# Two corners of causal attention, one product for two heads instead of one for each

## The chip, the cores and the metric

The kernel runs on one core of one Trainium2 chip. The metric is the device time of one execution in microseconds (us); lower is better. Before the change it is 387.51 us, the median of 3 runs (386.67 to 387.80).

The core's engines each work through their own queue in order: TensorE (PE: matrix products, with its weight loads as PEld), VectorE (DVE), ScalarE (ACT), GpSimd (POOL) and SyncE (SP), which issues the DMAs here.

## The reference

Per batch and head (8 x 8 heads, 576 positions, head size 64) causal attention with a decay, then a soft mixture of experts over all 4608 tokens:

```
scores = scale * q @ k^T
cum    = cumsum(log(clip(f, 1e-4, 1)))
scores = where(causal, -1e9, scores + cum_i - cum_j)
attn   = exp(scores - rowmax);  attn /= attn.sum + 1e-9
x      = (attn @ v), heads side by side         # 4608 x 512
logits = x @ phi;  dispatch = softmax over tokens;  combine = softmax over slots
out    = combine @ experts(dispatch^T @ x)      # two layers with relu
```

## The kernel before

**Tiling.** The 64 heads are worked as 32 pairs `g`, 4 pairs to a batch. For a pair, `YA` holds the rounded queries of both heads with extra rows below them (constants, and one row of row maxima), and `WA` the rounded keys with rows of the decay's sums; `YB` and `WB` hold copies and rounding remainders. All in float32r.

**Three stages per head.**

- `s1` and `tops` find each query's largest score. `s1` (L225) puts queries on partitions, blocks of 128 that are shifted by 64: block 0 is 64 blank lanes and the first 64 queries, blocks 1 to 4 are whole. Causality bounds the keys of a block: 64, 192, 320, 448 and 576 (as 2 x 288), six products in four fills of PSUM banks `s` (there are three such banks). `tops` (L238, DVE) adds a mask and reduces each product to a column of `MT`. `mturn` (L248) transposes a pair's ten columns, `mrows` copies them on ACT and sends them by DMA as the row of maxima into `YA`.
- `s2` and `expo` make the weights, with keys on partitions. `SEGS` lists six segments of a head: key blocks 0, 1, 2 with 320, 448, 320 queries, block 0 again with 256, block 3 with 192, and block 4 with 64 keys and 64 queries. Each is two products (L275 with `WA`/`YA`, L276 with the remainders). Four of the segments open a bank of `ring` (three banks); the last three share one. `expo` (L282, ACT) writes the exponentials of a bank to `PT`, and `causal` (L290, L293, POOL) clears the triangles.
- `s3` (L308) multiplies the weights with V, 50 products per pair, each seen twice in the trace; `norm` divides.

**Order.** It is written out by hand: the code's order is each engine's order. Iteration `g` of the main loop (g = 1 to 31) does `s2` for heads h0 = 2g and h1 = 2g+1, between them `s1` and `tops` for u0 = 2g+3 (second head of pair g+1) and u1 = 2g+4 (first head of pair g+2), the transposes of pair g-1, and at its end `s3` of pair g. So a row maximum is made a pair ahead of its use. POOL makes remainders (`low_q`, `low_k`) and the triangles. Every fourth iteration adds the batch's logits (L380), every fourth the dispatch (L461). Weights of the experts are loaded behind it; the tail after the loop computes the experts and stores the output.

**Before the loop** pair 0 and the first half block work of pairs 1 and 2 run with waits between engines, among them `both` (that is `s2` and `expo` of one bank) and `first` (`s1` and `tops`).

Of the kernel before, what the change touches and what calls it, by code (L numbers as in the profile page):

```python
# [41 lines left out]
SEGS = (  # L42
    (0, 1, 128, 448),
    (1, 0, 0, 320),
    (2, 2, 256, 320),
    (3, 0, 320, 256), (3, 3, 384, 192), (3, 4, 512, 64),
)
SEG_O = (640, 0, 320, 1088)


def pt_col(c, i):
    at = {}
    for bank, cc, i0, w in SEGS:
        o = at.get(bank, 0)
        at[bank] = o + w
        if cc == c and i0 <= i < i0 + w:
            return SEG_O[bank] + o + i - i0
    raise ValueError


def queries(t, u):
# [4 lines left out]
HALF = [  # L66
    [(h, t, u, c) for h in range(2) for t in ((4, 3, 2, 1, 0), (0, 1, 2, 3, 4))[h] if t < 4 or u == h for c in range(queries(t, u) // 2 + 1)]
    for u in range(2)
]
VALUES = [x for n in range(25) for h in HALF for x in h[n : n + 1]]  # L70

@with_exitstack
def attn_softmoe(ctx: ExitStack, tc: tile.TileContext, qk, v, f, phi, w1, w2, cst, out):
# [12 lines left out]
    cumd = dram.tile([2, NG, 2, S], F32, name="cumd")  # L86
# [5 lines left out]
    mask = fr[1].tile([P, 448], F32, name="mask")  # L92
    YA, WA, YB, WB = {}, {}, {}, {}
    for n, m in enumerate((1, 0, 2)):
        YA[m] = fr[n].tile([P, 2, 640], F32R, name=f"YA{m}")
        WA[m] = fr[n].tile([P, 2 * S], F32R, name=f"WA{m}")
        if m < 2:
            YB[m] = fr[n].tile([P, 2, S], F32R, name=f"YB{m}")
            WB[m] = fr[n].tile([P, 2 * S], F32R, name=f"WB{m}")
    RAW = [per.tile([P, 2, S], F32, name=f"RAW{i}") for i in range(3)]  # L100
    PTS = per.tile([P, 3200], F32, name="PTS")
    PT = [PTS[:, 1600 * i : 1600 * i + 1600] for i in range(2)]
# [12 lines left out]
    MT = [const.tile([P, 2 * NBLK], F32, name=f"MT{i}") for i in range(3)]  # L115
# [33 lines left out]
    def pair(g):  # L149
        return 0 <= g < NG  # L150
# [29 lines left out]
    def round_q(g, *hs):  # L180
        if pair(g):
            for h in hs or range(2):
                nc.scalar.copy(YA[g % 3][0:64, h, 64:640], RAW[g % 3][0:64, h])  # L183

    def load_cum(g):
        if pair(g):
            r0, r1 = CUM[g % 3]
            dst = WA[g % 3][r0 : r1 + 1 : r1 - r0, 0 : 2 * S].rearrange("c (h s) -> c h s", h=2)
            nc.sync.dma_start(dst.bitcast(F32), cumd[:, g].rearrange("h c s -> c h s"))
# [6 lines left out]
    def dup_q(g, h0=0, h1=2):  # L196
        if pair(g):
            nc.sync.dma_start(YB[g % 2][0:64, h0:h1].bitcast(F32), YA[g % 3][0:64, h0:h1, 64:640].bitcast(F32))
# [7 lines left out]
    def low_q(i):  # L206
        if head(i):
            g, h = divmod(i, 2)
            nc.gpsimd.tensor_tensor(YB[g % 2][64:128, h], RAW[g % 3][0:64, h], YA[g % 3][0:64, h, 64:640].bitcast(F32), op=ALU.subtract)  # L209


    TOPS = ((0, 0, 2, 0, 320), (0, 320, 1, 0, 192), (1, 0, 4, 0, 288), (2, 0, 4, 288, 288), (3, 0, 3, 0, 448), (3, 448, 0, 0, 64))

    def s1(i, *which):
# [4 lines left out]
        ya, wa, m = YA[g % 3], WA[g % 3][:, S * h : S * h + S], TOP[g % 3]  # L219
        for n in which:  # L220
            bank, o, blk, j0, w = TOPS[n]
# [3 lines left out]
            nc.tensor.matmul(  # L225
                t[:, o : o + w], ya[0:m, h, 128 * blk : 128 * blk + 128], wa[0:m, j0 : j0 + w], start=True, stop=True
            )

    def tops(i, *which):
# [3 lines left out]
        for n in which:  # L233
            bank, o, blk, j0, w = TOPS[n]
            t = st["top", i % 2, bank]
            m0 = max(448 - (128 * blk + 64) + j0, 0)
            top = MT[g % 3][:, NBLK * h + blk : NBLK * h + blk + 1] if g else m2[h][:, blk, 1:2]
            nc.vector.tensor_tensor_reduce(  # L238
                out=t[:, o : o + w], in0=t[:, o : o + w], in1=mask[:, m0 : m0 + w], scale=1.0, scalar=top if n == 3 else -3.0e38,
                op0=ALU.add, op1=ALU.max, accum_out=top,  # L240
            )

    def mturn(g, h0=0, h1=2):
# [4 lines left out]
        nc.tensor.transpose(pm[0 : NBLK * (h1 - h0), 0:128], MT[g % 3][:, NBLK * h0 : NBLK * h1], ident)  # L248
        st["pm", g, h0] = pm

    def mrows(g, h0=0, h1=2):
# [3 lines left out]
        n = NBLK * (h1 - h0)  # L255
        mr = small.tile([2 * NBLK, P], F32R, name=f"mr{g}_{h0}", tag="mr", bufs=1)
        nc.scalar.copy(mr[0:n], st["pm", g, h0][0:n, 0:128])  # L257
        m = TOP[g % 3]
        dst = YA[g % 3][m : m + 1, h0:h1].rearrange("c h s -> c (h s)")
        nc.sync.dma_start(dst.bitcast(F32), mr[0:n].bitcast(F32))  # L260

    def s2(i, *which):
# [4 lines left out]
        for n in which:  # L267
            bank, c, i0, w = SEGS[n]
            t, at = (turn(), 0) if n < 4 else st["bank"]

            n = 128 if c < 4 else 64
            o = t[0:n, at : at + w]
            at += w
            j0 = S * h + 128 * c
            nc.tensor.matmul(o, wa[0:m, j0 : j0 + n], ya[0:m, h, 64 + i0 : 64 + i0 + w], start=True, stop=False)  # L275
            nc.tensor.matmul(o, wb[:, j0 : j0 + n], yb[:, h, i0 : i0 + w], start=False, stop=True)  # L276
# [7 lines left out]
    def causal(i):  # L284
# [3 lines left out]
        pt = PT[i % 2]  # L288
        d3 = pt[:, 0:960].rearrange("p (a b) -> p a b", b=320)[:, :, 0:128]
        nc.gpsimd.affine_select(d3, d3, pattern=[[0, 3], [1, 128]], compare_op=ALU.is_ge, fill=0.0, base=0, channel_multiplier=-1)  # L290
        for o, w in ((pt_col(3, 384), 128), (pt_col(4, 512), 64)):
            dd = pt[:, o : o + w]
            nc.gpsimd.affine_select(dd, dd, pattern=[[1, w]], compare_op=ALU.is_ge, fill=0.0, base=0, channel_multiplier=-1)  # L293
# [9 lines left out]
    def s3(g, values):  # L303

        for h, t, u, c in values:
            r = queries(t, u)
            at = pt_col(c, 64 * r)
# [771 lines left out]
```

## Time and profile before

| | |
|---|---|
| median of 3 runs | 387.51 us |
| profiled execution | 386.95 us |
| its span, first to last instruction | 385.2 us |
| PE busy | 94% of the span |
| DVE, ACT, POOL busy | 73%, 69%, 67% |
| mean granted clock | 0.984 |

The profile is of one execution, whose own time is 1.75 us longer than the span. Busy shares are averages over the start (about 27 us), the loop and a tail from about 330 us on, in which the weights stream in at some 400 GB/s. PE's products overlap in a pipeline and their ends are modelled, so the chain of waits, which counts from end to end, says better than a mean duration what one product costs.

### The profile page before, as it was taken

The numbers are of one execution on the slowest core, as the hardware profiler recorded it, in microseconds if no ns is written. First come the engines' busy times: TensorE is split into PE (matmuls) and PEld (weight loads), VectorE is DVE, ScalarE is ACT, GpSimd is POOL, SyncE is SP. The second block draws the span as 40 slices with busy tenths as digits, with TensorE's granted clock in tenths as the row PEclk, the third lists the DMA queues.
The fourth block names the chain that finished last, engine by engine and source line by source line (L and its number), as shares of the span: only waits on it lengthen the run. The fifth ranks groups of instructions, "written<-read, shape, count | busy, mean of one in ns | idle before, by whom it ended". The sixth has DMA issues, their size and how long they took to land.

```text
span 385.2 us, 15103 instructions
## 1 busy us (share of the span) xinstructions
PE 362.4 (94%) x5795; PEld 325.5 (84%) x5795; DVE 281.0 (73%) x1133; ACT 266.2 (69%) x671; POOL 258.7 (67%) x378
## 2 busy tenths in 40 slices
PE   8989999999999999999999999999999998998940
PEld 7879999999999999999999999999999875443620
DVE  7778887889788978888888788878978443412741
ACT  8887787878787878787878778787876553011631
POOL 3887888878878888788878887888788621000000
PEclk9999999999999999999999999999999999999985
DMA  6875667687868777777777777868675799999997
GB/s 207 223 159 156 180 188 208 188 239 223 261 183 254 219 229 213 222 216 215 217 217 216 215 224 212 229 208 236 208 188 154 258 365 378 409 406 403 346 359 300
DMA packets 35144, 93.72 MB, mean 243 GB/s; under 512 B 4234, under 2 KB 10048, under 8 KB 35072
## 3 DMA queue, kind: packets, MB, share of 16 engines
q1 hardware_dynamic: 35072, 92.75, 77.4%
q8 instruction: 46, 0.75, 0.8%
q14 instruction: 26, 0.21, 0.2%
HBM read 63.93 MB, written 9.73 MB: 191 GB/s over the span
## 4 chain that ended last, share of the span: by engine, by line
PE 84%; DMA 9%; DVE 1%; ACT 1%; SPq 1%; issue 1%; DVEq 0%; ACTq 0%
PE pv L308 24%; PE ring L275 15%; PE ring L276 13%; PE s L225 13%; DMA w<-in_w 5%; PE pv L334 4%; PE lg L380 2%; DMA out<-p 2%; PE ds L461 2%; PE ring L498 2%; DMA YA<-mr 2%; PE more L894 1%; PE pv L894 1%; PE pv L498 1%; PE pv L931 1%
## 5 line engine op out<-in xcount | busy, mean ns | idle before, releaser
L282 ACT ACTIVATE PTS<-ring 128x320 f32<-128x320 f32 (+2 forms) x256 | 118.6, 502 | 46.2 <-PE ring L276 39.2
L238 DVE CUSTOM_DVE_ANT_0 s<-s,mask 128x320 f32<-128x320 f32 (+4 forms) x320 | 138.1, 452 | 7.1 <-PE s L225 2.1
L275 PE MATMUL ring<-YA,WA 67*128 67x320 f32 (+9 forms) x384 | 121.7, 329 | 0.5 <-DMA YA<-mr 0.5
L276 PE MATMUL ring<-YB,WB 128*128 128x320 f32 (+4 forms) x384 | 110.5, 296 | 0.0
L308 PE MATMUL pv<-V,PTS 128*64 128x65 f32 x3200 | 101.7, 223 | 0.4 <-ACT mr L257 0.3
L308 PEld LDWEIGHTS pv<-V,PTS 128*64 128x64 f32 x3200 | 96.9, 138 | 3.2 <-issue 0.9
L204 POOL TENSOR_TENSOR WB<-RAW,WB 64x576 fp32r<-64x576 f32 x64 | 90.4, 1414 | 11.8 <-ACT YA L183 5.6
L225 PE MATMUL s<-WA,YA 66*128 66x288 f32 (+9 forms) x384 | 96.3, 306 | 0.5 <-DVE MT L238 0.3
L209 POOL TENSOR_TENSOR YB<-RAW,YA 64x576 fp32r<-64x576 f32 x64 | 89.8, 1421 | 2.5
L275 PEld LDWEIGHTS ring<-YA,WA 67*128 67x128 f32 (+3 forms) x384 | 69.1, 181 | 5.7 <-issue 1.6
L276 PEld LDWEIGHTS ring<-YB,WB 128*128 128x128 f32 (+1 forms) x384 | 69.9, 182 | 0.0
L225 PEld LDWEIGHTS s<-WA,YA 66*128 66x128 f32 (+1 forms) x384 | 64.0, 190 | 3.7 <-DVE MT L238 0.5
L238 DVE DVE_READ_ACCUMULATOR2_ANT MT<- 128x1 f32 x372 | 52.8, 142 | 0.0
L293 POOL TENSOR_SCALAR_AFFINE_SELECT PTS<-PTS 128x128 f32<-128x128 f32 (+1 forms) x128 | 31.5, 268 | 25.8 <-ACT PTS L282 23.0
L178 ACT CAST WA<-RAW 64x576 fp32r<-64x576 f32 x64 | 40.0, 669 | 6.9 <-DMA RAW<-in_qk 6.3
L290 POOL TENSOR_SCALAR_AFFINE_SELECT PTS<-PTS 128x384 f32<-128x384 f32 x64 | 33.4, 522 | 13.8 <-ACT PTS L282 8.7
L183 ACT CAST YA<-RAW 64x576 fp32r<-64x576 f32 x64 | 40.1, 670 | 0.5
L238 DVE CUSTOM_DVE_ANT_0 s<-s,mask,MT 128x288 f32<-128x288 f32 x62 | 32.6, 526 | 9.6 <-PE s L225 0.9
L334 PE MATMUL pv<-cs,X 128*128 128x128 f32 x155 | 37.0, 273 | 0.6 <-DVE X L327 0.6
L327 DVE TENSOR_TENSOR X<-pv,rl 128x320 f32<-128x320 f32 (+1 forms) x65 | 31.6, 487 | 2.4 <-DMA YA<-mr 0.3
L322 DVE TENSOR_SCALAR rl<-pv 128x5 f32<-128x5 f32 x64 | 10.5, 164 | 25.0 <-PE pv L308 24.3
L369 ACT COPY XT<-pv 128x128 f32<-128x128 f32 (+1 forms) x93 | 25.0, 307 | 0.6 <-PE pv L334 0.6
(184 smaller groups left out, 345.7 us busy)
## 6 DMA issues: line engine op xcount, KB each, us to landing
w<-in_w SPq DMA_DIRECT2D x46, 512.0 KB
RAW<-in_qk SPq DMA_DIRECT2D x31, 576.0 KB
V<-in_v SPq DMA_DIRECT2D x32, 325.0 KB
WB<-WA SPq DMA_DIRECT2D x31, 288.0 KB
YB<-YA SPq DMA_DIRECT2D x31, 288.0 KB
p<-in_w SPq DMA_DIRECT2D x7, 512.0 KB
out<-RAW SPq DMA_DIRECT2D x12, 256.0 KB
out<-p SPq DMA_DIRECT2D x5, 512.0 KB
```

Source lines behind the costliest of these rows:

```text
L178: nc.scalar.copy(WA[g % 3][0:64, S * h : S * h + S], RAW[g % 3][64:128, h])
L183: nc.scalar.copy(YA[g % 3][0:64, h, 64:640], RAW[g % 3][0:64, h])
L204: nc.gpsimd.tensor_tensor(t[0:64], RAW[g % 3][64:128, h], t[64:128].bitcast(F32), op=ALU.subtract)
L209: nc.gpsimd.tensor_tensor(YB[g % 2][64:128, h], RAW[g % 3][0:64, h], YA[g % 3][0:64, h, 64:640].bitcast(F32), op=ALU.subtract)
L225: nc.tensor.matmul(t[:, o : o + w], ya[0:m, h, 128 * blk : 128 * blk + 128], wa[0:m, j0 : j0 + w], start=True, stop=True)
L238: nc.vector.tensor_tensor_reduce(out=t[:, o : o + w], in0=t[:, o : o + w], in1=mask[:, m0 : m0 + w], scale=1.0, scalar=top if n == 3 else ...
L275: nc.tensor.matmul(o, wa[0:m, j0 : j0 + n], ya[0:m, h, 64 + i0 : 64 + i0 + w], start=True, stop=False)
L276: nc.tensor.matmul(o, wb[:, j0 : j0 + n], yb[:, h, i0 : i0 + w], start=False, stop=True)
L282: nc.scalar.activation(PT[i % 2][:, SEG_O[bank] : SEG_O[bank] + at], t[:, 0:at], AF.Exp, scale=0.125)
L290: nc.gpsimd.affine_select(d3, d3, pattern=[[0, 3], [1, 128]], compare_op=ALU.is_ge, fill=0.0, base=0, channel_multiplier=-1)
L308: nc.tensor.matmul(pvv[h][64 * u : 64 * u + 64, t, :], PT[h][:, at : at + 64], V[:, g % 2, c, 65 * h : 65 * h + 65], start=(c == 0), stop= ...
L334: nc.tensor.transpose(pm[:, 0:128], x[:, t, p % 2, 0:128], ident)
```

## The change

The queries of each first head are stored rotated, so that its first 64 stand last, right before the first 64 of the second head; the keys of each second head are rotated the other way, so that its last 64 stand first, right behind the last 64 of the first head. With that:

- the two 64 x 64 products of row-maximum block 0 become one product `base`, 128 queries (64 of each head) by 128 keys (64 of each), under a mask that also shuts out the pairs of unlike heads; one DVE reduction `btops`; nine columns in `MT`;
- the two last segments of `s2` become `corner`, two products of 128 x 128 for both heads in a `ring` bank of its own, of which `cexpo` takes the two diagonal 64 x 64 pieces with two ACT instructions into `PC`, and `ccausal` clears their triangles with one POOL instruction. The off-diagonal pieces of `PC` stay zero;
- the second head's block 4 is cut as 192 + 384 keys instead of 288 + 288, so that `base` finds room beside the 384;
- `expo` of the last bank is 448 wide instead of 512; `causal` has four POOL instructions for the first head (it had three) and two for the second (three).

`base(g+2)` runs in the first half of iteration g, `corner(g)` at the end of that half. Before the loop, `base(1)` stands ahead of the second head's `s2`, and `corner(0)`, `cexpo(0)` between its second and third bank. The rotated sums of the decay need three more DMAs and two more ACT copies there; blank columns and some memsets go.

```diff
+def qcol(h, i):
+    return S + i if h else i - 64 if i >= 64 else 512 + i
+def kcol(h, j):
+    return j if h == 0 else 640 + j if j < 512 else 64 + j
...
-    (1, 0, 0, 320),
-    (3, 0, 320, 256), (3, 3, 384, 192), (3, 4, 512, 64),
+        (1, 0, 0, 320) if h else (1, 0, 320, 320),
+        (3, 0, 320 if h else 64, 256), (3, 3, 384, 192),
...
-    TOPS = ((0, 0, 2, 0, 320), (0, 320, 1, 0, 192), (1, 0, 4, 0, 288), (2, 0, 4, 288, 288), (3, 0, 3, 0, 448), (3, 448, 0, 0, 64))
+            (1, 0, 4, 512, 192) if h else (1, 0, 4, 0, 288), (2, 0, 4, 128, 384) if h else (2, 0, 4, 288, 288),
...
+    def base(g, t):
+        m = TOP[g % 3]
+        st["base"] = t[:, 384:512]
+        to = st["base"].rearrange("p (h s) -> p h s", h=2)
+        nc.tensor.matmul(to, YA[g % 3][0:m, 512:640], pieces(WA[g % 3])[0:m, 0::5, 0:64], start=True, stop=True)
+    def btops(g):
+            nc.vector.tensor_tensor_reduce(
+                out=t, in0=t, in1=mask[:, 448:576], scale=1.0, scalar=-3.0e38, op0=ALU.add, op1=ALU.max, accum_out=MT[g % 3][:, 4:5]
+            )
+    def corner(g):
+        t = st["corner"] = turn()
+        m = TOP[g % 3] + 1
+        to = t[:, 0:128].rearrange("p (h s) -> p h s", h=2)
+        nc.tensor.matmul(to, WA[g % 3][0:m, 512:640], pieces(YA[g % 3])[0:m, 3::5, 64:128], start=True, stop=False)
+        nc.tensor.matmul(to, WB[g % 2][:, 512:640], pieces(YB[g % 2])[:, 3::5, 64:128], start=False, stop=True)
+    def cexpo(g):
+        for h in range(2):
+            d = slice(64 * h, 64 * h + 64)
+            nc.scalar.activation(PC[d, d], st["corner"][d, d], AF.Exp, scale=0.125)
+    def ccausal(g):
+        nc.gpsimd.affine_select(PC, PC, pattern=[[1, 128]], compare_op=ALU.is_ge, fill=0.0, base=0, channel_multiplier=-1)
...
+    base(1, turn())
+    btops(1)
     causal(0)
...
         s1(u0, 3)
+        if g > 1 and head(u0):
+            base(g + 2, st["top", 1, 2])
         tops(u0, 3)
+        if g > 1:
+            btops(g + 2)
...
         s2(h0, 4)
-        s1(u0, 4, 5)
-        s2(h0, 5)
+        s1(u0, 4)
+        corner(g)
         expo(h0, 3)
-        tops(u0, 4, 5)
+        cexpo(g)
+        tops(u0, 4)
         causal(h0)
+        ccausal(g)
...
         s2(h1, 3, 4)
-        s1(u1, 4, 5)
+        s1(u1, 4)
         mturn(g + 1)
-        s2(h1, 5)
         mrows(g + 1)
         expo(h1, 3)
-        tops(u1, 4, 5)
+        tops(u1, 4)
```

How PE's order moves, in one iteration of the loop (`ring` are the banks of `s2`, `s_1` and `s_2` those of `s1`). Early in the first half, before:

```order
L225 MATMUL s_1_2313<-WA_84,YA_83 128x288
L275 MATMUL ring_148<-YA_87,WA_88 128x320
L276 MATMUL ring_148<-YB_89,WB_90 128x320
L225 MATMUL s_2_2319<-WA_84,YA_83 128x288
L275 MATMUL ring_149<-YA_87,WA_88 128x320
L276 MATMUL ring_149<-YB_89,WB_90 128x320
```

and there now:

```order
L252 MATMUL s_1_2826<-WA_84,YA_83 128x192
L341 MATMUL ring_147<-YA_87,WA_88 128x320
L342 MATMUL ring_147<-YB_85,WB_86 128x320
L252 MATMUL s_2_2832<-WA_84,YA_83 128x384
L285 MATMUL s_2_2832<-WA_92,YA_91 128x128
L341 MATMUL ring_148<-YA_87,WA_88 128x320
```

The two halves of 288 have become 192 and 384, and `base` (L285) of the pair after the next follows the 384 in the same bank. At the end of the first half, before:

```order
L276 MATMUL ring_147<-YB_89,WB_90 128x192
L225 MATMUL s_3_2340<-WA_84,YA_83 128x448
L225 MATMUL s_3_2340<-WA_84,YA_83 128x64
L275 MATMUL ring_147<-YA_87,WA_88 64x64
L276 MATMUL ring_147<-YB_89,WB_90 64x64
L275 MATMUL ring_148<-YA_87,WA_88 128x448
```

and now:

```order
L342 MATMUL ring_149<-YB_85,WB_86 128x192
L252 MATMUL s_3_2855<-WA_84,YA_83 128x448
L299 MATMUL ring_147<-YA_87,WA_88 128x128
L300 MATMUL ring_147<-YB_85,WB_86 128x128
L341 MATMUL ring_148<-YA_87,WA_88 128x448
```

Three narrow products have gone and the two of `corner` (L299, L300) have come, in a bank of their own. At the end of the second half, before:

```order
L276 MATMUL ring_148<-YB_89,WB_90 128x192
L225 MATMUL s_3_2380<-WA_92,YA_91 128x448
L225 MATMUL s_3_2380<-WA_92,YA_91 128x64
L248 MATMUL pv_146<-cs,MT_111 10x128
L275 MATMUL ring_148<-YA_87,WA_88 64x64
L276 MATMUL ring_148<-YB_89,WB_90 64x64
L308 MATMUL pv_145<-V,PTS 64x65 x21
```

and now:

```order
L341 MATMUL ring_148<-YA_87,WA_88 128x192
L342 MATMUL ring_148<-YB_85,WB_86 128x192
L252 MATMUL s_3_2897<-WA_92,YA_91 128x448
L317 MATMUL pv_146<-cs,MT_111 9x128
L385 MATMUL pv_145<-V,PTS 64x65 x21
```

Three narrow products have gone and none has come; the transpose of the maxima stands right ahead of `s3`.

## Rows read from the trace of the kernel before

**Rows 1.** The page: busy time by engine, and the chain's shares by engine.
```profile
PE 362.4 (94%) x5795; PEld 325.5 (84%) x5795; DVE 281.0 (73%) x1133; ACT 266.2 (69%) x671; POOL 258.7 (67%) x378
...
PE 84%; DMA 9%; DVE 1%; ACT 1%; SPq 1%; issue 1%; DVEq 0%; ACTq 0%
```

**Rows 2.** Busy time in three successive iterations: stretch and length, engines, granted clock, DMA.
```profile
109.85:119.78 9.93, 9.93 (x187) 9.46 (x183) 8.26 (x34) 7.91 (x21) 8.29 (x11) 1.00 0.84 234
119.78:128.46 8.68, 8.68 (x146) 8.41 (x143) 7.81 (x34) 7.00 (x19) 7.00 (x11) 1.00 0.70 216
128.46:138.26 9.80, 9.80 (x178) 9.31 (x175) 8.18 (x34) 7.63 (x19) 8.79 (x11) 1.00 0.81 229
```

**Rows 3.** Chain of waits from 100 to 122 us: start, us added, what.
```profile
110.97 0.14 PE s L225
...
112.31 0.09 PE ring L275
112.41 0.11 PE ring L276
112.52 0.25 PE s L225 x2
112.77 0.06 PE ring L275
112.83 0.06 PE ring L276
112.89 0.29 PE ring L275
113.17 0.20 PE ring L276
...
114.22 0.15 PE ring L276
114.37 0.24 PE s L225 x2
114.61 0.15 PE ring L275
114.76 0.12 PE ring L276
...
115.08 0.26 PE s L225 x2
115.34 0.11 PE pv L248
115.45 0.03 PE ring L275
115.48 0.06 PE ring L276
```

**Rows 4.** ACT in the same iteration, in order of time: start, us, instruction, idle before.
```profile
113.01 1.03 ACT L282 ACTIVATE PTS<-ring 128x512 f32<-128x512 f32 x2 [0.71 <-PE ring L276]
...
114.18 0.43 ACT L343 COPY XT<-pv 64x64 f32<-64x64 f32 x2
```

**Rows 5.** Waits of all engines from 30 to 330 us: total, times, longest.
```profile
PE ring L275 <- DMA YA<-mr: 0.5, 1, 0.5
```

**Rows 6.** PE before the loop, in order of time.
```profile
17.46 1.18 PE L498 MATMUL pv<-cs 128*128 128x184 f32 x6
18.35 0.49 PE L275 MATMUL ring<-YA,WA 98*128 98x448 f32 x1
...
23.19 0.47 PE L225 MATMUL s<-WA,YA 66*128 66x320 f32 x2 [0.17 <-DMA YA<-mr]
```

**Rows 7.** ACT before the loop, in order of time.
```profile
17.94 0.67 ACT L183 CAST YA<-RAW 64x576 fp32r<-64x576 f32 x1
19.13 0.94 ACT L282 ACTIVATE PTS<-ring 128x448 f32<-128x448 f32 x2 [0.52 <-ACT YA L183]
...
22.32 1.25 ACT L183 CAST YA<-RAW 64x576 fp32r<-64x576 f32 x2
```

**Rows 8.** DVE at the loop's start, in order of time.
```profile
27.85 0.23 DVE L238 CUSTOM_DVE_ANT_0 s<-s,mask 128x64 f32<-128x64 f32 x1
...
28.42 0.49 DVE L327 TENSOR_TENSOR X<-pv,rl 128x320 f32<-128x320 f32 x1
```

More of the change, by code (lines that the diff above doesn't have):

```diff
@@ L40, with pt_col @@
 ORDER = [8 * e + k + n for e, k in STEPS for n in range(2 if k else 4)]
[L42 to L51 removed]
+SEGS = [
+    (
+        (0, 1, 128, 448),
+        (1, 0, 0, 320) if h else (1, 0, 320, 320),
+        (2, 2, 256, 320),
+        (3, 0, 320 if h else 64, 256), (3, 3, 384, 192),
+    )
+    for h in range(2)
+]
+SEG_O = (640, 0, 320, 1088)
+PTW = 1536
+def qcol(h, i):
+    return S + i if h else i - 64 if i >= 64 else 512 + i
+def kcol(h, j):
+    return j if h == 0 else 640 + j if j < 512 else 64 + j
+def pt_col(h, c, i):
     at = {}
[L53 removed]
+    for bank, cc, i0, w in SEGS[h]:
         o = at.get(bank, 0)
         at[bank] = o + w
[L56 to L57 removed]
+        n = qcol(h, i) - qcol(h, i0)
+        if cc == c and 0 <= n < w:
+            return SEG_O[bank] + o + n
     raise ValueError
@@ L63, in queries, with half @@
     return 2 * t + u if t < 4 else 8
[L66 to L70, printed above, removed]
+def half(u):
+    return [(h, t, u, c) for h in range(2) for t in ((4, 3, 2, 1, 0), (0, 1, 2, 3, 4))[h] if t < 4 or u == h for c in range(queries(t, u) // 2 + 1)]
+VALUES = [x for both in zip(half(0), half(1)) for x in both]
 @with_exitstack
@@ L114, in attn_softmoe @@
     mk = const.tile([P, NE], F32, name="mk")
-    MT = [const.tile([P, 2 * NBLK], F32, name=f"MT{i}") for i in range(3)]
+    MT = [const.tile([P, 9], F32, name=f"MT{i}") for i in range(3)]
     quarter = [wres.tile([P, QW], F32, name=f"w{n}") for n in range(NRES)]
@@ L287, in causal, with keep @@
             return
[L288 to L293, printed above, removed]
+        h = i % 2
+        pt = PT[h]
+        def keep(at, w, base=0, n=1):
+            dd = pt[:, at : at + 320 * n].rearrange("p (a b) -> p a b", b=320)[:, :, 0:w] if n > 1 else pt[:, at : at + w]
+            nc.gpsimd.affine_select(
+                dd, dd, pattern=[[0, n], [1, w]][n == 1 :], compare_op=ALU.is_ge, fill=0.0, base=base, channel_multiplier=-1
+            )
+        if h:
+            keep(0, 128, n=3)
+        else:
+            keep(320, 128, n=2)
+            keep(pt_col(0, 0, 0), 64)
+            keep(pt_col(0, 0, 64), 64, base=64)
+        keep(pt_col(h, 3, 384), 128)
     def blank(n):
@@ L637, in attn_softmoe @@
     nc.sync.dma_start(phis, phi)
-    nc.sync.dma_start(mk, cst[:, 706:714])
+    nc.sync.dma_start(mk, cst[:, 962:970])
+    corner(0)
+    cexpo(0)
+    ccausal(0)
     both(1, 2)
@@ L656, in attn_softmoe @@
     first(4, 1)
+    base(2, turn())
+    btops(2)
     s3(0, alone[1][:13])
@@ L761, in attn_softmoe @@
         s1(u1, 3)
+        if g == 1:
+            base(3, st["top", 0, 2])
         tops(u1, 3)
+        if g == 1:
+            btops(3)
         s2(h1, 2)
```

160 lines of the change are left out of this document (95 added, 65 removed).

## The prediction

> **What bounds the kernel now.** I read the page first. PE is busy 94% of the span, and the chain that ended last is 84% PE [rows 1]; the other engines have a quarter to a third of the span free. An average can hide stages, so the busy time of whole iterations came next. In three successive ones, 9.93, 8.68 and 9.80 us long, PE is busy for the whole of each, at a granted clock of 1.00, which is the 2.4 GHz level; DVE has 0.9 to 1.7 us free, ACT 1.7 to 2.2, POOL 1.0 to 1.7 [rows 2]. The loop is PE's own work with no wait in it. So the change is worth what it does to PE's order, as long as no other engine falls behind. The third view is the chain inside one iteration, which gives the price of each product from the end of the one before [rows 3].
>
> **How products are priced.** Behind a long product a product costs its columns: 0.20 us for 448, 0.15 for 320, 0.14 for 288, 0.09 for 192 behind a 256, which is some 0.47 ns a column [rows 3]. Behind a short one it costs more. A 192 right behind a 192 takes 0.11 and not 0.09; a 256 behind a 192 takes 0.15 where the next 256 takes 0.12; and the 448 behind a product of 64 columns takes 0.29 where the next 448 takes 0.20 [rows 3]. In all three, a product with 128 columns of weights starts about 0.11 us after the one before it started, however few columns that one streamed (0.29 - 0.20 + 0.03 for the 64's own columns is 0.12; 0.15 - 0.12 + 0.09 is 0.12). The 64-wide products, with 64 columns of weights, follow each other at 0.06 [rows 3]. The load of the next weights sets this floor: 0.11 for 128 columns, 0.06 for 64.
>
> **The change on PE, per iteration.** The columns stay the same in sum (two times 64 against 128, 576 against 192 + 384); the narrow products change their kind.
> - Early in the first half, 288 and 288 cost 0.14 + 0.14 = 0.28 or a little less (0.27 with the next digit of 0.13 to 0.14). Now 192 costs the floor of 0.11 before its successor starts, 384 lies between 320 and 448, 0.18, and `base`, whose 128 columns stream in 0.06, costs the floor of 0.11. Together 0.40: plus 0.13.
> - At the end of the first half, 448 and 64 (0.25), two 64-wide products (0.06 each) and the following 448 (0.29) are 0.66. Now 448 alone is 0.22 (0.25 less 0.03 for the 64), the first `corner` product 0.06 with its weights loaded under the 448, the second 0.11, and the 448 behind it 0.20 + 0.11 - 0.06 = 0.25, in sum 0.64 to 0.66: about minus 0.01.
> - At the end of the second half the 64 behind the 448 goes (0.03: 0.26 less the 0.23 of a 448 behind a 192) and the two 64-wide products go (0.03 + 0.06): minus 0.12 [rows 3]. What is late next is `s3`, which starts that much earlier; its first operands are of the first half.
>
> The sum is 0.13 - 0.01 - 0.12 = 0.00, with some 0.02 of rounding. For 29 iterations with a `base` I take 0.1 us in all. No row shows a 128-column product of this type; its price lies between its columns alone, 0.06, and that of a 192 with its successor's wait, 0.12, and I take the floor, 0.11, which three different pairs of rows show. The moving operand of `base` and `corner` is two pieces of 64, which no row shows either; at no cost or at a gap of 0.03 (the price of a 64) each, three a pair, this is 0 to 2.6 us; I take 0, because the columns are read from the same partitions.
>
> **The other engines.** DVE loses two 64-wide reductions of 0.23 (plus their read-outs) and gets one of 128: it gains, hidden. ACT gets two 64 x 64 instructions, 0.43 us for a pair of that shape [rows 4], and its 512 becomes 448, 0.05 less for each head: plus 0.33 per iteration of which ACT has at least 1.7 free [rows 2]. Behind the two on ACT's queue stands the `expo` of the second head's first bank. Before, the 512 began at 113.01 after 0.71 idle, waiting for the 64-wide products [rows 4]; now the 448 needs only the 192 that ended at 112.52 [rows 3], so ACT starts some 0.3 sooner and ends the pair at about 113.7, within 0.2 of when that `expo` began before. PE needs its bank again four segments later, at 114.61 [rows 3], some half a microsecond after. POOL gets one instruction more and the same area; it has 1.0 us free [rows 2]. Price of the others: 0.
> `base(g+2)` needs pair g+2's keys, queries and sums, which were needed in the second half before and now a good 2 us earlier; the casts are done in ACT's queue ahead of this iteration's first `expo`, so they are there. The row of maxima leaves less room: PE reaches the next iteration 0.09 sooner after `mturn`. PE waited for this DMA once in the loop, 0.5 us [rows 5], so 0.1 of a saving can be lost there; it is in the rounding.
>
> **Before the loop.** `base(1)` needs both heads' queries, whose cast ended at 18.61 [rows 7]; the second head's `s2` began at 18.35 [rows 6] and now stands behind it, some 0.2 to 0.4 late. ACT's chain from there (the `expo` at 19.13, then casts to 23.57 [rows 7]) gets `cexpo`, 0.4, before the casts that release PE at 23.19 [rows 6]. So PE's restart there is 0.4 late, or up to 0.8. But at the loop's start DVE sets the pace: its division ends at 28.91, behind a 64-wide reduction of 0.29, read-out included, that goes [rows 8]. That takes back about 0.3. The three extra DMAs stand in SP's queue at 10 to 12 us, where it has waits behind them. I take plus 0.1, between minus 0.3 and plus 0.8. The tail is unchanged.
>
> **Sum.** 0.1 + 0.1 = 0.2 us on the profiled execution's 386.95 (span 385.2 and 1.75 around it), 387.15. That execution lies 0.56 under the median of the runs, 387.51; with that the forecast is 387.7 us.
>
> **Rivals.**
> - *Faster: weights don't set the pace.* If a 128-column product costs less than the 0.11 floor, the first half doesn't lose what the second gains. At columns alone, 0.06, the first half costs 0.33 instead of 0.27 early and 0.55 instead of 0.66 at its end: 0.06 - 0.11 - 0.12 = -0.17 per iteration, 29 of them -4.9 us, 382.8. Halfway it is -2.4, 385.3. For it speaks that loads may run ahead; against it that none of the three pairs of rows shows a 128-wide load under the floor. Chance 0.15.
>   The Trainium skill, same page, section "Back-to-back issue gap", gives about 81 ns per product at 128 columns in a stream of loads and products. By that, three products a pair would be 0.03 cheaper than the floor, by estimate 29 x 0.09 = 2.6 us, near the halfway case. The same page's section "LDWEIGHTS (loading the stationary operand)" gives the columns over 1.2 as the time of a load, 107 ns for 128, by which nothing is gained. The trace's 0.11 for a 192 behind a 192 agrees with the second and not with the first.
> - *Slower: nine turns of three banks.* `corner` takes a bank, and with ACT's 0.33 more the second head's `s2` waits for `expo`. The point is the half microsecond between ACT's freeing a bank and PE's need of it: were `cexpo` held up by 0.6 instead of 0.2, each iteration would wait 0.1, 29 of them 2.9 us: 390.6. The same would come of moving operands in two pieces at 0.03 each. Against it: ACT's free 1.7 us. Chance 0.20, with the case that the start isn't absorbed and PE's rounding goes against me (0.8 + 29 x 0.02 = 1.4: 388.9).
> - *Nothing moves*: the sum lies within 0.3 us. This is the forecast. Chance 0.65.
>
> **How the numbers follow.** A measurement of this kernel can tell about 0.3% (1.2 us) from no change. Faster has the first rival, 0.15, slower the second, 0.20, the same 0.65. The likeliest case alone holds 386.8 to 388.6. For 8 in 10 the range goes down to the halfway price of the first rival, 385.4, and up through the unabsorbed start to 389.6.
>
> **What would show it.** In the chain after: 0.11 for the second `corner` product and 0.25 for the 448 behind it; `base` with its successor near 0.2; plain iterations still 8.68 us with PE busy throughout. Iterations of 8.5 would show the first rival; PE idle behind ACT in the second half the second. A loop start later than 26.83 + 0.5 would show the start not absorbed.

## The result, and the profile after

The changed kernel takes 390.07 us, the median of 13 runs, against 387.29 for the kernel before in as many; the ratio of times is 1.0066 [1.0038 to 1.0094]. It is 2.6 us slower, where no change was forecast. Some executions of it, and of several variants below, take 391.5 to 399.7 us, most with a lower mean granted clock; the ratios leave most of these out, the medians don't, and the profiled execution shown here, 394.77 us with a span of 393.1, is one of them.

The page of the profile after, as [rows 1], with the granted clock of TensorE in 40 slices between:

```profile
PE 368.9 (94%) x5700; PEld 322.0 (82%) x5700; DVE 274.7 (70%) x1068; ACT 276.0 (70%) x737; POOL 261.4 (67%) x408
...
PEclk9997999999999999999999999999999999999985
...
PE 76%; DMA 13%; ACT 3%; issue 1%; DVE 0%; POOL 0%; ACTq 0%; DVEq 0%; SPq 0%
```

PE has 95 products fewer and is as busy as before. DMA has gone from 9% of the chain to 13% and ACT from 1% to 3%. The clock dips in the fourth slice, at 29 to 39 us, where it had stood at 9.

Three successive iterations of the loop, busy time as in [rows 2], here cut from one `mturn` to the next; the first has L457's products and the third L538's:

```profile
103.30:113.39 10.09, 10.09 (x175) 9.36 (x174) 7.77 (x33) 8.11 (x23) 8.86 (x16) 1.00 0.81 254
113.39:122.06 8.67, 8.67 (x140) 8.16 (x139) 6.88 (x30) 7.64 (x22) 7.48 (x12) 1.00 0.65 174
122.06:132.08 10.02, 10.02 (x181) 9.26 (x179) 8.23 (x34) 7.84 (x22) 7.79 (x12) 1.00 0.82 254
```

PE is still busy for the whole of each, and a plain iteration takes 8.67 against 8.68. The long ones of [rows 2] are cut elsewhere; the table below compares these. The chain of waits, as [rows 3], around `corner` (L299, L300) and around `base` (L285):

```profile
100.93 0.06 PE ring L299
100.99 0.11 PE ring L300
101.10 0.25 PE ring L341
...
108.77 0.18 PE s L252
108.95 0.06 PE s L285
109.02 0.20 PE ring L341
```

For `corner` and the 384 these are the prices of the prediction to the hundredth: 0.06 for the first `corner` product, 0.11 for the second, 0.25 for the 448 behind, 0.18 for the 384. `base` and the 320 behind it are 0.06 and 0.20 where the working had 0.11 and 0.15, the same sum. So the loop is not where most of the time went. The time from one `mturn` to the next, by the four kinds of iteration (medians within a trace, their mean over the traces, worked out from the starts of L248 and L317 between the third and the last but one):

```
                                  plain  with L538  plain  with L457
6 traces with the old products    8.69   9.93       8.69   10.09
9 traces with the new ones        8.69   9.96       8.71   10.10
```

Seven times these four come to 261.74 us with the old products (261.71 to 261.75) and 262.0 to 262.6 with the new, 0.45 us more in the mean. The 28 iterations of a single trace, with what they hold of single waits of up to 1.5 us, take 260.6 to 262.3 with the old products and 261.3 to 263.4 with the new; beside that, 0.45 is small.

Before the loop, SP's queue is what changed. The issues of the kernel after, in order of time (start, us, instruction, times):

```profile
9.08 2.35 SPq L630 DMA_DIRECT2D WA<-PTS  x3
11.47 1.94 SPq L633 DMA_DIRECT2D cumd<-PTS  x3
...
15.38 0.58 SPq L187 DMA_DIRECT2D RAW<-in_qk  x1
16.09 0.36 SPq L191 DMA_DIRECT2D V<-in_v  x1
17.05 0.33 SPq L187 DMA_DIRECT2D RAW<-in_qk  x1
```

and the same of the kernel before:

```profile
9.18 1.12 SPq L551 DMA_DIRECT2D WA<-PTS  x2
10.36 0.50 SPq L552 DMA_DIRECT2D cumd<-PTS  x1
...
12.89 0.58 SPq L169 DMA_DIRECT2D RAW<-in_qk  x1
13.88 0.34 SPq L173 DMA_DIRECT2D V<-in_v  x1
16.02 0.33 SPq L169 DMA_DIRECT2D RAW<-in_qk  x1
```

Six small transfers in the place of three push the 576 KB of `RAW[2]` from 12.89 to 15.38 and the 325 KB of V from 13.88 to 16.09; the next 576 KB go out 1.0 later. 0.5 of the 2.5 us is no slot but a wait: the third write of pair 1's sums is held until an earlier load of `RAW` has landed.

```profile
SPq L630 <- DMA RAW<-in_qk: 0.5, 1, 0.5
```

In the trace of the changed kernel run again this wait is 1.8 us and `RAW[2]` leaves at 16.71; in e2 and e3 below, which make the same six writes, there is none and it leaves at 14.81 and 14.90. What the later bulk does to the chain (after, then before):

```profile
21.10 6.79 DMA YA<-mr
...
27.98 0.26 ACT mr L326
...
28.38 2.18 PE pv L385 x26
```

```profile
20.33 2.80 DMA YA<-mr
23.86 0.26 ACT mr L257
24.26 1.23 PE pv L308 x26
```

The row of maxima of pair 1's first head, 2.5 KB, lands 6.79 us after its issue, where it took 2.80. ACT's next copy into `mr` waits for it (`mr` has one buffer), and PE's `s3` waits for that copy: its 26 products begin at 28.38 and not at 24.26. They also take 2.18 and not 1.23. The stretches of 2 us around it (after; columns as above, the clock is the third number from the end):

```profile
24.00:26.00 2.00, 0.66 (x10) 0.55 (x8) 0.00 (x0) 0.86 (x2) 0.00 (x0) 1.00 1.02 177
26.00:28.00 2.00, 0.54 (x5) 0.37 (x4) 1.65 (x8) 0.01 (x1) 1.42 (x2) 1.00 0.59 129
28.00:30.00 2.00, 1.62 (x23) 1.65 (x24) 0.00 (x0) 1.97 (x4) 1.93 (x2) 0.53 0.01 2
30.00:32.00 2.00, 2.00 (x17) 1.47 (x15) 0.79 (x4) 0.76 (x2) 2.00 (x2) 0.50 0.94 187
```

From 24 to 28 us PE is busy for 1.20 of 4.00 us (3.74 before the change), with the DMA engines full for the first half of that time, and then the clock stands at half, the 1.2 GHz level, until about 35 us. The third `mturn` comes at 39.60; before the change it came at 33.01.

### The profile page after: what moved, and what is told of

Its sections match the earlier page's. It is cut to its first block, busy times and chain, and to the rows that moved or that the text cites. A ratio compares the mean times of both kernels' runs of the same rounds, so it can differ in the third digit from the quotient of the medians.

```text
span 393.1 us, 15011 instructions
## 1 busy us (share of the span) xinstructions
PE 368.9 (94%) x5700; PEld 322.0 (82%) x5700; DVE 274.7 (70%) x1068; ACT 276.0 (70%) x737; POOL 261.4 (67%) x408
## 4 chain that ended last, share of the span: by engine, by line
PE 76%; DMA 13%; ACT 3%; issue 1%; DVE 0%; POOL 0%; ACTq 0%; DVEq 0%; SPq 0%
PE pv L385 25%; PE ring L341 14%; PE ring L342 12%; PE s L252 11%; DMA w<-in_w 8%; PE pv L411 4%; DMA YA<-mr 2%; PE lg L457 2%; DMA out<-p 2%; PE ds L538 2%; PE ring L300 1%; DMA out<-RAW 1%; PE pv L317 1%; PE more L993 1%; ACT PTS L348 1%
## 5 line engine op out<-in xcount | busy, mean ns | idle before, releaser
L348 ACT ACTIVATE PTS<-ring 128x448 f32<-128x448 f32 (+1 forms) x256 | 118.0, 488 | 44.6 <-PE s L252 19.7
L269 DVE CUSTOM_DVE_ANT_0 s<-s,mask 128x192 f32<-128x192 f32 (+3 forms) x258 | 120.7, 492 | 6.9 <-PE s L252 4.0
L341 PE MATMUL ring<-YA,WA 98*128 98x448 f32 (+4 forms) x320 | 110.4, 351 | 0.3 <-DMA YA<-mr 0.3
L342 PE MATMUL ring<-YB,WB 128*128 128x320 f32 (+3 forms) x320 | 97.2, 311 | 0.0
L252 PE MATMUL s<-WA,YA 66*128 66x192 f32 (+5 forms) x322 | 94.6, 329 | 1.8 <-DMA YA<-mr 1.3
L360 POOL TENSOR_SCALAR_AFFINE_SELECT PTS<-PTS 128x256 f32<-128x256 f32 (+2 forms) x192 | 60.4, 331 | 40.1 <-ACT PTS L348 31.3
L341 PEld LDWEIGHTS ring<-YA,WA 67*128 67x128 f32 (+1 forms) x320 | 61.1, 191 | 5.4 <-issue 1.4
L342 PEld LDWEIGHTS ring<-YB,WB 128*128 128x128 f32 x320 | 61.4, 192 | 0.0
L269 DVE CUSTOM_DVE_ANT_0 s<-s,mask,MT 128x288 f32<-128x288 f32 (+1 forms) x62 | 35.7, 576 | 12.1 <-PE s L252 3.6
L411 PEld LDWEIGHTS pv<-cs,X 128*128 128x128 f32 x155 | 21.8, 141 | 1.1 <-PE ring L342 0.3
```

The lines of the kernel that those rows point to most:

```text
L252: nc.tensor.matmul(t[0:lanes, o : o + w], ya[0:m, a : a + lanes], wa[0:m, k : k + w], start=True, stop=True)
L269: nc.vector.tensor_tensor_reduce(out=t[rows, o : o + w], in0=t[rows, o : o + w], in1=mask[rows, m0 : m0 + w], scale=1.0, scalar=top if n = ...
L341: nc.tensor.matmul(o, wa[0:m, k : k + 128], ya[0:m, q : q + w], start=True, stop=False)
L342: nc.tensor.matmul(o, wb[:, k : k + 128], yb[:, q : q + w], start=False, stop=True)
L348: nc.scalar.activation(PT[i % 2][:, SEG_O[bank] : SEG_O[bank] + at], t[:, 0:at], AF.Exp, scale=0.125)
L360: nc.gpsimd.affine_select(dd, dd, pattern=[[0, n], [1, w]][n == 1 :], compare_op=ALU.is_ge, fill=0.0, base=base, channel_multiplier=-1)
```

## The experiments

Ratios are to the kernel before, run on the same chip. "Third `mturn`" is its start in the profiled execution, the end of what a kernel loses before and at the loop's start; before the change it is 33.01.

```
                        median  ratio                    third mturn
changed kernel again    390.03  1.0066 [1.0040, 1.0091]  36.97
e1 bulk first           389.53  1.0089 [1.0057, 1.0120]  33.90
e2 cut alone            392.92  1.0087 [1.0048, 1.0126]  35.70
e3 products later       389.77  1.0081 [1.0051, 1.0111]  34.58
e7 e1 + copies' order   388.87  1.0035 [0.9997, 1.0072]  33.58
e5 e7 + products later  390.63  1.0072 [1.0038, 1.0106]  37.75
e8 early load           388.91  1.0055 [1.0033, 1.0078]  34.28
e9 early load, before   386.25  0.9998 [0.9970, 1.0026]  33.33
e11 e2 + products       393.72  1.0184 [1.0142, 1.0226]  38.42
e16 idle transfers      394.80  1.0235 [1.0196, 1.0275]  44.34
e17 cut, behind bulk    387.77  1.0032 [1.0012, 1.0053]  33.40
e18 POOL's queue        388.83  1.0047 [1.0029, 1.0066]  33.37
e4 e1 + base late       391.49  1.0117 [1.0087, 1.0148]  33.77
e13 base late, ds bank  390.92  1.0098 [1.0070, 1.0125]  33.24
```

**Cut the transfers, keep the old products (e2).** In the kernel before:

```diff
-for c in range(2):
-    nc.sync.dma_start(WA[1][64 + c : 65 + c]..., fp[65:98:32, S * c : S * c + S]...)
-nc.sync.dma_start(cumd...)
+for h, j, w in RUNS: nc.sync.dma_start(WA[1][64:66, ...]...)       # 3 pieces
+for h, j, w in RUNS: nc.sync.dma_start(cumd[h, :, :, j : j + w]...)  # 3 pieces
```

> The kernel before with one thing added: its two transfers of pair 1's sums and its one write of the sums to DRAM are cut into three each, as in the changed kernel; nothing else of the change. Theory A: the start is late by most of the changed kernel's loss, about 2 us, 389.2 us, 0.4 to 0.6% above the kernel before, and the loads of RAW[2], V and RAW[3] go out some 2.4 us later. Theories B and C: the products are as before, so the time is as before, 387.3.

This alone costs 0.87%, and 7 of 12 runs lie above 391.5 us; two of the seven are in the ratio, and without them it would be 0.59%, the upper end of what was expected. Busy time in e2, whose profiled execution is one of the five others:

```profile
24.00:26.00 2.00, 0.71 (x4) 0.53 (x4) 0.78 (x3) 0.12 (x1) 0.72 (x1) 1.00 0.77 150
26.00:28.00 2.00, 1.73 (x27) 1.63 (x27) 0.62 (x4) 1.95 (x4) 2.00 (x2) 0.72 0.10 29
```

The idle stretch and the fall of the clock come without any new product, so this much of what happens before the loop is the transfers' alone: the row of maxima lands 5.55 us after its issue.

**The slots without the cut (e16), and the cut without the slots (e17).** In the kernel before, e16 writes one 4.5 KB row of pair 1's sums three times more, with the same values, ahead of the uncut `cumd`; e17 is e2 with the three writes of `cumd` moved behind `load_v(0)`.

```diff
 # e16
+for _ in range(3):
+    nc.sync.dma_start(WA[1][65:66]..., fp[65:98:32, S : 2 * S]...)
 nc.sync.dma_start(cumd...)
 # e17
-for h, j, w in RUNS: nc.sync.dma_start(cumd[h, :, :, j : j + w]...)
 ...
 load_v(0)
+for h, j, w in RUNS: nc.sync.dma_start(cumd[h, :, :, j : j + w]...)
```

> The kernel before with nothing cut, but with three more transfers of 4.5 KB at the place where the change has three more: they write one row of pair 1's sums again, with the same values. Only the time that three issues take on SP's queue, some 1.9 us, is added ahead of the bulk. If the place in the queue is the cause (theories A and E: the bulk goes out 1.9 us later onto engines that are full from 16 us on), it costs what the cut cost in e2: 388 to 389.7 in most runs, and some runs at 392 to 398 with the clock down. If the cut pieces are the cause (smaller descriptors, three writes to DRAM), it is as the kernel before, 387.

> e2 (the kernel before with its transfers cut) with the three writes of the sums behind the loads of RAW[2] and V, as e1 does in the changed kernel. With the old products this shows what that order is worth without the change's work on PE and ACT. If the bulk's place is the cause: at most 0.2% above the kernel before, no run above 391. If the pieces are: as e2, 0.5 to 0.9% above.

SP's issues in e16, where the added writes are L553:

```profile
9.18 1.13 SPq L551 DMA_DIRECT2D WA<-PTS  x2
11.44 3.67 SPq L553 DMA_DIRECT2D WA<-PTS  x3
15.16 0.49 SPq L554 DMA_DIRECT2D cumd<-PTS  x1
...
17.69 0.59 SPq L169 DMA_DIRECT2D RAW<-in_qk  x1
```

and in e17:

```profile
12.95 0.58 SPq L169 DMA_DIRECT2D RAW<-in_qk  x1
13.70 0.33 SPq L173 DMA_DIRECT2D V<-in_v  x1
14.07 1.80 SPq L568 DMA_DIRECT2D cumd<-PTS  x3
```

e16 is an overdose: each added write waits for the one before it, so the bulk is 4.8 us late and not 1.9, the row of maxima lands 7.21 us after its issue, and the loss is 8 us in the median and 6.6 or more in every run, not the 1 to 2 expected. It is not a clean test either: PE waits 0.7 us for the added writes themselves, ahead of the idle stretch. What it shows is that writes ahead of the bulk cost time with nothing cut. e17 is the cleaner one, from the other side. All pieces are cut, the bulk goes out at its old time, and no run of 12 is above 389.75 where 7 of e2's 12 are above 391.5; 0.32% is left of e2's 0.87%, more than the 0.2% expected. So the pieces themselves don't bring most of the loss; their place ahead of the bulk does. (The intervals of the two ratios overlap at their ends; the runs above 391.5 and the traces carry the verdict.)

**The same in the changed kernel (e1, e8, e18).** e1 moves the writes of `cumd` behind `load_v(0)`; e8 issues `load_qk(2)` at 9 us; e18 lets POOL issue the writes. e8 and e18 also have e7's order of copies, below.

```diff
 # e1: the writes moved as in e17
 # e8
     dup_k(0, 1, 2)
+    load_qk(2)
 ...
-load_qk(2)
 load_v(0)
 # e18
-                nc.sync.dma_start(cumd[:, :, k : k + w], ...)
+                nc.gpsimd.dma_start(cumd[:, :, k : k + w], ...)
```

> The changed kernel with one thing moved: the three transfers that write the sums of all pairs to DRAM stand in SP's queue behind the loads of RAW[2] and of V for pair 0, not ahead of them. Theory A (SP's queue: the three extra DMAs hold up the three bulk loads by 2.3 to 2.5 us, and these then stand in front of the small transfers WB, YB, sums and maxima that PE waits for): the bulk loads go out at about their old times, 13 and 14 us, the row of maxima lands some 3 us after its issue and not 6.8, the loop starts near 27 us, and the time falls by 2 to 2.5 us to 387.5 to 388.1, 0 to 0.2% above the kernel before; the granted clock shows no fall before the loop. Theory B (PE's and ACT's order before the loop: base(1), corner(0) and cexpo(0) stand ahead of work that PE waits for): nothing changes, 390. Theory C (the loop itself is dearer by 0.025 us an iteration, 0.7 us in all): the part that stays above the kernel before is 0.7 us, 388.0.

> The changed kernel with the load of RAW[2], 576 KB, which waits for nothing, issued at 9 us, ahead of the sums, and with ACT's small copies in the order of e7. Theory E (what matters is when the bulk gets onto the 16 DMA engines: they work 52 of 64 engine-us between 12 and 16 us in the kernel before, 25 in the changed one and 39 with the bulk first, and all of them are full from 16 us on, so every byte that isn't moved before 16 us is late behind it, and the last of them is the row of maxima): the engines are busy from 9 us, the row of maxima lands at 23 us or before, third mturn at 33.0 to 33.4, no run with a fallen clock (none above 391), and the time is the loop's 0.6 to 0.9 us above the kernel before. Theory A (only the order of the queue counts): no better than e7, 0.35% above. If PE's idle stretch stays, theory E is wrong.

> The changed kernel with its three writes of the sums issued by POOL, which has nothing to do from 8 to 10 us, and not by SP, and ACT's copies in the order of e7. The writes go out at the old time, 9 to 12 us, while the engines are idle, and SP's bulk loads go out 1.9 us sooner than in the changed kernel. If SP's place is the cause: the row of maxima lands by 23.5 us, third mturn at 33.1 to 33.5, and the time is the loop's 0.45 us (0.016 an iteration) and 0.2 to 0.5 us of the start above the kernel before, 0.15 to 0.25%; no run above 391. If the pieces or the products are: no better than e7.

The three writes in e18, on POOL, and PE's `s3` in the stretch that stood idle:

```profile
8.88 1.70 POOL L633 DMA_DIRECT2D cumd<-PTS  x3 [4.91 <-DVE PTS L616]
```

```profile
24.00:26.00 2.00, 1.81 (x31) 1.63 (x30) 1.64 (x8) 1.80 (x4) 2.00 (x2) 1.00 0.29 87
26.00:28.00 2.00, 2.00 (x29) 1.65 (x28) 1.45 (x7) 1.25 (x3) 1.93 (x3) 1.00 0.73 144
```

In e18's trace the idle stretch is gone, the row of maxima lands by 23.6 us, the third `mturn` is 0.36 us late, and one run of 12 is above 391.5 (4 of 13 in the changed kernel and 2 of 10 in it run again, too few to tell apart). As far as its trace's start goes it did what was expected. The time did not: 0.47% and not 0.15 to 0.25, an interval that still overlaps the changed kernel's. e1 and e8 stay above as well, at 0.89 and 0.55%, though their starts are only 0.9 and 1.3 late; e1's time did not fall by the 2 to 2.5 us expected. In e8, V still waited for constant rows that now stood behind the writes, and the row landed at 24.8, so the expectation of 23 failed. Over these three the start as traced explains a fifth to three fifths of what is left.

The Trainium skill's "DMA: Bandwidth & Descriptors", section "Issuing engines are not separate DMA queues", says that issuing from several engines saves only the sequencer's time, which is usually small beside the transfer. e18 agrees with the first half: with the three writes on POOL, `RAW[2]` leaves SP at 12.87 and not 15.38. On the second, a slot of 0.54 to 0.64 us is small beside the 2.4 to 2.9 us in which e18's writes land; but what three more slots of 0.39 to 0.65 us cost the kernel in e2, 0.87%, is not small.

**The clock (e11).** e2 with `warm(18, cs)` ahead of `first(4, 0)`: products that nothing reads, in PE's idle stretch.

```diff
 s3(0, alone[0])
+warm(18, cs)
 first(4, 0)
```

> e2 (the kernel before with its three transfers cut in three) with 18 products that nothing reads on PE, about 2.9 us, in the stretch at 22.6 us in which PE waits for the row of maxima and the sums of pair 2. If the clock falls because PE stands idle there, the runs at 392 to 398 us, 6 of 12 in e2, are gone and the rest, 388.0 to 389.7, stays, since the row comes no sooner. If something else lowers the clock, half of the runs are still above 391.5.

```profile
26.00:28.00 2.00, 2.00 (x15) 2.00 (x14) 0.00 (x0) 0.00 (x0) 1.26 (x1) 1.00 0.27 70
28.00:30.00 2.00, 1.66 (x16) 1.47 (x15) 0.87 (x5) 0.72 (x2) 1.93 (x3) 1.00 0.00 0
```

Each such product shows as two, so the 18 took 5.9 us and not 2.9, and the real work starts later still; the time is worse than expected, 393.7. But the clock holds at 1.00 in the trace, and the six runs lie within 2 us (392.9 to 394.9), where e2's lie within 10. That PE's idle stretch is what lowers the clock in e2 is borne out. A trace of the changed kernel run again adds the price: PE was busy 0.78 of 2.00 at 26 us there, the clock stayed at 1.00, and with the row landing at the same time as above (27.99 against 27.89) the third `mturn` came at 36.97 and not at 39.60. The fall costs 2.6 us in that pair. It is not all that makes a run long: this second execution takes 394.84 us as well, for it lost 2.1 us more in the loop, in single stops of PE, and 0.6 behind it.

**ACT's copies, and the products' place (e7, e3, e5, e14).** The change's front has two more ACT copies before the loop, four pieces for two rows. They stood as high, low, high, low, and each low part waits for DVE. After, then e7, where both high parts come first:

```profile
8.65 1.49 ACT L638 CAST WA<-PTS 1x64 fp32r<-1x64 f32 x3 [0.62 <-DVE PTS L616]
10.17 0.67 ACT L201 CAST YA<-RAW 64x576 fp32r<-64x576 f32 x1
```

```profile
7.78 1.62 ACT L635 CAST WA<-PTS 1x64 fp32r<-1x64 f32 x4
9.43 0.67 ACT L201 CAST YA<-RAW 64x576 fp32r<-64x576 f32 x1
```

```diff
-    for h, j, w in RUNS[1:]:
-        for r in range(2):
+    for r in range(2):
+        for h, j, w in RUNS[1:]:
```

> The bulk-first kernel (e1) with ACT's four small copies of pair 0's sums in another order: both of the high parts first, which are ready, then both of the low parts, which wait for DVE until 8.55 us. Nothing else moves. Theory D: the copies end at 9.5 and not at 10.14 us (9.41 in the kernel before); ACT's casts, the first s2 and base(1) come 0.6 us sooner, third mturn at 33.3 to 33.5 against e1's 33.9, and the time is 0.4 to 0.6 us under e1, 389.0 us on e1's chip. Theory A alone: as e1, since ACT has time there.

The cast behind them starts at 9.43, as before the change (9.44), and not at 10.17; third `mturn` is 33.58 against e1's 33.90. 0.3 us is just short of the expected 0.4 to 0.6; the ratios of e1 and e7, from two chips, fall by 0.5% with overlapping intervals. But 4 of e7's 10 runs lie above 391.5, at mean granted clocks of 0.958 to 0.978 (0.983 in the traced one), where none of e1's 6 does. Its trace shows no such run, so why they fell stays open. e3 puts `base(1)` behind `both(1, 0)`, and `corner(0)`, `cexpo(0)`, `ccausal(0)` behind `round_q(2)`:

```diff
-    base(1, turn())
-    btops(1)
 ...
     both(1, 0)
+    base(1, turn())
+    btops(1)
 ...
-    corner(0); cexpo(0); ccausal(0)
     both(1, 2)
 ...
     round_q(2)
+    corner(0); cexpo(0); ccausal(0)
```

> The changed kernel with its products before the loop moved back: base(1) behind the first s2 of pair 0's second head, and corner(0), cexpo(0) and its causal mask behind round_q(2); SP's queue is left as it is. Theory A: what PE waits for comes from SP's queue, so the loop starts as late as before the move, 390.0 us (389.5 to 390.5). Theory B: the cast of pair 2's queries and PE's restart come 0.4 to 0.8 us sooner and most of the loss goes, 388 us.

389.77, as theory A had it. Its third `mturn`, 34.58, is sooner than in either trace of the changed kernel, but SP's wait of 0.5 or 1.8 us is not in it, so the two orders can't be compared by that. e5 is e7 and e3 together:

> All three repairs of the start in one kernel: bulk loads first on SP's queue, ACT's copies in the order of e7, and base(1), corner(0), cexpo(0) behind the work that PE and ACT wait for. The loop is that of the changed kernel. Expected by the theory that the start has these three causes and no other: third mturn at 33.0 us as before the change, and what remains above the kernel before is the loop's, 0.6 to 0.9 us, 0.15 to 0.25%. If the loss lies elsewhere (the loop at the chip's own pace, the tail), it stays 2 us or more above.

It was to bring the start back and failed: third `mturn` at 37.75 and 5 of 10 runs above 391.5. PE came to the idle stretch sooner (first `mturn` at 19.46, before the change 19.44), waited there longer, busy 0.33 of 2.00 us from 24 on, and the clock fell. Here the bulk leaves at 13.05 and 13.76, as before the change, and the row of maxima still lands 7.14 us after its issue: a bulk in time is not enough. What else holds the row up no run isolates. The same order on a start like e8's with V sooner (e14) gave 1.0069:

> e12 with base(1) behind the first s2 of the second head and corner(0), cexpo(0) behind the cast of pair 2's queries, as in e3. In e5 this order brought mturn(1,0) back to 19.46, its time before the change, but the transfers were late and PE waited. If they come in time here, third mturn is at 33.0 as before the change and what stays is the loop's 0.02 us an iteration, 0.6 us, 0.15%; if the row of maxima lands after 24 us, it is no better than e12.

It began its third `mturn` at 39.32, the clock down again; the row landed at 25.7, and by its second case it is no better than e12 (1.0065). While the transfers set the start, PE's order ahead of them brought nothing in these three.

**The price of `base` (e4, e13).** e4 is e1 with `base(g+2)` moved from between two products with 128 columns of weights to the place behind `mturn`, ahead of `s3`.

```diff
-        if g > 1 and head(u0):
-            base(g + 2, st["top", 1, 2])
 ...
         mturn(g + 1)
+        base(g + 2, st.get(("top", 0, 2)))
```

> The bulk-first kernel (e1) with base(g+2) moved in the loop: not between two products with 128 columns of weights, but at the end of the iteration before, behind mturn and ahead of the 64-wide products of s3, whose weights are 64 columns. If the load of the next product's weights is what makes a 128-column product cost 0.11 us, base costs its columns there, 0.06: 28 iterations with 0.05 less each, 1.4 us below e1, about 386.3 us, which is 0.25% below the kernel before. If the price lies in the product itself (its two pieces of 64), it costs the same at its new place: e1's time.

The chain around its old place in e1, then the new in e4, with the 320 whose weights it had held up:

```profile
93.40 0.06 PE s L285
93.46 0.20 PE ring L341
```

```profile
89.25 0.06 PE s L285
89.31 3.07 PE pv L385 x100
...
93.57 0.15 PE ring L341
```

The 320 is back at 0.15 and the plain iterations at 8.64 (8.71 in e1): `base` costs its successor 0.05 where that has 128 columns of weights and nothing where it has 64, as a load of weights would. As a version it lost: 1.0117. The iterations with L538's products rose from 9.98 to 10.45; PE waited there 6 times, 3.1 us, by the trace for ACT's copy into `mr`. That the PSUM bank which `base` now holds is what L538's products lack is my reading of the order. Two other banks lost 0.3 and 0.6 us in those iterations: the ring's (e6, 10.29 against e5's 9.95; 1.0100), and in e13, on e8's start with V sooner, the bank of L538's own product:

> e12 with base(g+2) behind mturn and ahead of s3 in a bank that is free, as in e10, whose profiled execution can't be read. Weights' theory: plain iterations 8.64 and the ones with L538's products 9.95, 1.0 to 1.4 us below e12. By what e4, e6 and e10 did in sum (each 2 us above the kernel they were made from) it is 2 us above e12, and then the trace must show which iterations are longer.

There PE waits for DVE, which reads that bank:

```profile
PE ds L285 <- DVE acc L544: 2.4, 5, 0.5
```

e10, as e13 on e8, ran at a third of its speed when profiled, and e12, e8 with V sooner, at a lower clock throughout, so only their ratios count: 1.0125 and 1.0065. e9 issues `load_qk(2)` early in the kernel before:

> The kernel before with the load of RAW[2] issued at 9 us, as in e8; nothing of the change. Theory E: the row of maxima and the sums of pair 2 land sooner, but PE's restart at 23.19 is also set by ACT's casts, which end at 23.56, so at most 0.5 us is gained; 386.9 to 387.4.

It is no faster (0.9998). No variant beat the kernel before. Two buffers for `mr`, so that ACT's copy need not wait for the row's transfer, I have not tried.

**The tail.** What e18 still lacks, 1.8 us, is 0.36 at the start by its trace and 0.45 in the loop by the medians. The rest is behind the loop. From the last `mturn` to the experts' first product (L894; L993) it is 20.8 us in four of the six traces with the old products, 21.5 in the one of before and 22.4 in e11; with the new ones 21.6 to 22.7 in nine, 22.2 in the mean, 1.3 us more than with the old ones, e11 aside. 0.3 us of that lie ahead of L538's products there, which begin 12.7 us after the last `mturn` and not 12.4 (12.8 in e11 and in the changed kernel run again, 13.3 in e18, with a wait for the row of maxima). The rest lies in these products themselves: 1.3 to 2.4 us where the traces with the old ones, e11 aside, take 0.8. From there on both kinds take 7.6 us, and before 8.3. PE in e18's tail, then in e11's, where L538 is L461:

```profile
318.46 0.74 PE L538 MATMUL ring<-X,LD 128*32 128x129 f32 x17 [0.64 <-issue]
```

```profile
323.36 0.42 PE L461 MATMUL ring<-X,LD 128*32 128x129 f32 x6 [0.86 <-issue]
```

This stop in the middle of L538's products, 0.5 to 1.4 us of what the profile calls `issue` (idle time that nothing it shows has ended), stands in eight of the nine (0.2 in the ninth). With the old products PE stops later, at L688, for 0.5 to 1.5 us, and all but before's lose nothing by it. But e11 has the stop where the new kernels have it, without a product of the change and with only 18 products more ahead of it; and e6, with the new products, has none there and takes 0.8. So the loss goes with the place at which the stop falls, not with what the change computes.

The profile names no releaser, but its records point to one. The page lists a queue `q8 instruction` with 45 packets of 16 KB, one for some 250 of PE's products and weight loads. Leaving out e10 and e12, PE has 20 such stops of over 0.3 us behind 36 us, in loop and tail, and every one ends 2.2 to 2.6 us after one of these packets starts. I read that as PE waiting for its own next instructions; no run was made to test it. What follows, the experts' weights coming in, varies by 3.7 us from trace to trace (60.0 to 63.7).

## Why the prediction was wrong

- *PE's prices and the loop:* right. Every product cost what was forecast, `base` together with its successor, and PE has no wait in the plain iterations. 0.00 per iteration, 0.1 us in all, is measured as 0.016, 0.45 us in all: within the rounding that the prediction named. One of its signs was wrong by its own working: `base` with its successor, 0.11 and 0.15, could not be near 0.2, and is 0.26.
- *The rivals:* e4 bears out that weights set the pace, and no product came cheaper, so the faster one is out. The slower one's place, ring turns in the loop, is out as well: ACT's `cexpo` costs 0.43 and the loop does not wait for it. That its 390.6 lies near the 390.07 measured is chance.
- *Before the loop:* this is the first step that failed: "The three extra DMAs stand in SP's queue at 10 to 12 us, where it has waits behind them." It put their cost at nothing because SP waits later on. It did not ask what else of SP's queue stands between them and that wait: two bulk loads that waited for nothing but their turn. Behind these the DMA engines have little or no spare time from 16 to 26 us (shares of 0.88 to 1.07), so a bulk that was 2.5 us late came back as 4 us at the row of maxima. In the kernel before, the cut transfers alone cost 0.87% (e2), and 0.32% once they stand behind the bulk (e17). The bound of +0.8 was worked from PE and ACT alone; its sign, a loop that starts over 0.5 late, is what the traces show. The measured lateness of the start is 4.0 and 6.6 us in the two traces of the changed kernel, both of runs near 394.8; in a run of 390 it must be less, about 0.8 by what loop and tail leave of 2.6 us, and no trace shows that run (e3's, of a run of 389.5, is 1.6 late).
- *ACT before the loop:* `cexpo` was counted, the two added copies were not. They and their wait for DVE are 0.73 us late on ACT; in time e7 got back 0.3.
- *"The tail is unchanged":* this is the second, and by size the larger in a run of 390: the code is unchanged, the time is not. It is 1.3 us, the largest part of what stays when the start is mended, nearly all of it a stop of PE that falls at another place in the program. e11 and e6 show that it does not come with the new products; that PE waits there for its instructions is read from the packets and not tested. No row of before could have told it.

## What to carry to other kernels

A small transfer costs its issue slot, 0.39 to 0.66 us here, to everything behind it on its queue. Before pricing added DMAs at nothing, find the next bulk load in that queue and the moment from which the DMA engines are full: what is not under way by then can arrive late by more than the slots (5.55 us and not 2.80 for e2's row, behind a bulk 1.9 late). And where PE is left to wait at a start, look at the clock behind the wait as well. Before blaming the change for a loss in code that it did not touch, look for the same loss in a variant without it: e11 had it.

## What the runs showed that I had not expected

- The same kernel, same start, has a time that jumps by 3 to 9 us: e2's runs lie at 388 to 390 and at 392 to 398, and with products in the idle stretch (e11) none does so. In none of the traces in which PE worked through that stretch did the clock fall there (e12's, at 0.85 throughout, aside); e7's four long runs are without a trace.
- While the copies from SBUF to SBUF (`WB`, `YB`) run, packets are slow: one of 4608 bytes takes some 360 ns, and 178 when only loads from DRAM run, by the packet records between 18 and 28 us of before.
- `base` holds up the product behind it by 0.05 us in every iteration. Each of the three other banks traced for it behind `mturn` won about that back and lost 0.3 to 0.6 us in one iteration of four; in two of them the trace names the reader of the bank.
